# First q/k tiles uncast over two hardware DMA queues, first V through GpSimd, and scores in two PSUM tiles

## The chip, the cores and the metric

The kernel runs on one core of a Trainium2 chip. The core has TensorE (PE, with its weight loads shown as PEld), VectorE (DVE), ScalarE (ACT), GpSimd (POOL) and SyncE (SP). Each has its own queue of instructions, worked off in order; they meet at semaphores. Data come from HBM by DMA transfers, which GpSimd issues through a software queue and SyncE and ScalarE through hardware queues. A transfer issued by GpSimd may change the type on the way. The metric is the device time of one execution in microseconds.

## The reference, cut to what matters

```python
B, H, S, D = 8, 8, 576, 64           # q, k, v: [B, H, S, D], fp32
scores = q @ k.T / sqrt(D)           # masked: block of 64 rows i sees blocks j <= i
attn = exp(scores - max); attn /= sum(attn)
x = (attn @ v) as [B, S, 512]        # heads side by side
h = relu(x.T @ w_tok1) @ w_tok2      # 576 -> 256 -> 576, along the sequence
u = x + h.T
out = u + relu(u @ w_ch1) @ w_ch2    # 512 -> 1536 -> 512, along the channels
```

## The kernel before, in words

The kernel goes over eight batches b. For each it does attention in two head groups (hg) of four heads, then the token mix, then the channel MLP up and down. All products are in bf16 with fp32 sums.

**The planner.** Nothing is issued where it is written. Every step is an `Op` with the engines it may run on, an estimated cost, what it depends on, and a priority (lower goes first). `Plan.run` (L55) plays the work through with these estimates, a common DMA line (`xfer` is the estimated transfer time) and free lists of PSUM banks (`take`, `give`), and emits the steps in the order in which they start. That order is then the order of each engine's queue; the semaphores are set by the framework from what each instruction reads and writes.

**Loads.** `load_qk` (L245) fetches k and q of one head group: a transfer from GpSimd that casts to bf16 (`kraw`, `qraw`, rings of three), then one 32x32 block transpose on DVE into `kT` and `qT`. The 576 positions lie as 32 a x 18 k (`NB` = 18), so a transfer brings 18 rows of 64 to each of 128 partitions. `load_v` (L272) fetches V in five tiles of 128 positions (the last has 64), heads side by side, into `v1`, which also has a column of ones. For batch 0 the five tiles come uncast over ScalarE's hardware queue into `vstage` (L282), and DVE casts them (L292); for the others GpSimd's transfers cast (L286). After the first loads GpSimd sends the token weights (L305), the first and second halves of `wc1` (L324), and `wc2` (L333), with the loads of the next batches between them.

**Scores.** Per head group there are three sets of scores of up to 512 columns for each of four heads (`SETS`), transposed (keys on the partitions), each with a contraction of 32 twice (`par`). The PSUM tile `sc` has four banks, one for each head. For batch 0 a set is made in two halves, heads 0 and 1 and heads 2 and 3 (`halves`, with bank notes "sc01" and "sc23" in the planner); for the others a set is one step that takes both notes. ScalarE takes exp of two heads at a time into `e_sb` (L389). Small fills then zero the masked blocks on the diagonal (L428), for batch 0 on DVE or GpSimd. A last set of both head groups together, the tail, covers positions 512 to 575, into `et_sb`.

**AV.** For each head 15 products of the exponentials with V (L454) fill one bank; the column of ones gives the row sums, DVE inverts them (L475) and scales into `x_sb` (L481). In the planner the AV of every head depends on all the exponentials of its group, on the tail's and on V. The other steps (`token_mix` L532 to L654, `channel_up` L676, `channel_up_mixed` L703, `channel_down` L742) take a bank from `mm` (3) or `ups` (1); AV takes `ups` first.

Of the kernel before, what the change touches and what calls it, by code (L numbers as in the profile page):

```python
# [10 lines left out]
FP32 = mybir.dt.float32  # L11
# [104 lines left out]
def kernel(  # L116
# [11 lines left out]
    nc = tc.nc  # L128
# [36 lines left out]
    vstage = sb.tile([128, 5, DM], FP32, name="vstage")  # L165
# [16 lines left out]
    P.pool("ups", ups)  # L182
    P.pool("mm", mm)

    def bank_of(note):
        return (mm if note["pool"] == "mm" else ups)[note["slot"]]
# [51 lines left out]
    def warm_up():  # L238
        def emit(o):
            nc.scalar.activation(warm, nc.const_aps.tensor(0.0, (128, 1), FP32), EXP)  # L240

        P.add("ACT", 1.5, emit, (), -1e5)


    def load_qk(b, hg):  # L245
        i = (2 * b + hg) % 3
        prio = 10 * b + 4 * hg - (100 if b == 0 else 0)
        done = []
        for n, (src, raw, dst) in enumerate(((k, kraw[i], kT[i]), (q, qraw[i], qT[i]))):
            def emit_load(o, src=src, raw=raw):  # L250
                nc.gpsimd.dma_start(  # L251
                    out=raw.rearrange("p k d -> p (k d)"),
                    in_=src[b, 4 * hg : 4 * hg + 4].rearrange("h (p k) d -> (h p) (k d)", p=32),
                )

            load = P.add("POOL", 0.66, emit_load, reuse(("raw", n, i)), prio + n, xfer=8 * 0.191)

            def emit(o, raw=raw, dst=dst):
                nc.vector.transpose(  # L259
                    dst[:, 0:S, :]  # L260
                    .rearrange("p s e -> p (s e)")
                    .bitcast(I32)
                    .rearrange("p (a k) -> p k a", k=NB),
                    raw.rearrange("p k d -> p (k d)").bitcast(I32).rearrange("p (k a) -> p k a", k=NB),
                )

            op = P.add("DVE", dve_cost(576), emit, [load] + reuse(("T", n, i)), prio)
            reads(("raw", n, i), op)
            done.append(op)
        return done  # L270

    def load_v(b):  # L272
        t = v1[b % 2]
        war = reuse(("v", b % 2))
        done = []
        for J in range(5):
            p = 128 if J < 4 else 64

            def emit(o, J=J, p=p):
                src = v[b, :, 128 * J : 128 * J + p, :].rearrange("h p d -> p h d")  # L280
                if b == 0:
                    nc.scalar.dma_start(  # L282
                        out=vstage[0:p, J].rearrange("p (h d) -> p h d", h=H), in_=src
                    )
                else:
                    nc.gpsimd.dma_start(out=t[0:p, J, :, 0:64], in_=src)  # L286

            if b == 0:
                op = P.add("ACT", 0.5, emit, war, -1e4 + J, xfer=p / 2 * 0.018)

                def emit(o, J=J, p=p):
                    nc.vector.tensor_copy(  # L292
                        t[0:p, J, :, 0:64], vstage[0:p, J].rearrange("p (h d) -> p h d", h=H)
                    )

                op = P.add("DVE", dve_cost(512, 2), emit, [op], 2)
            else:
                op = P.add("POOL", 0.66, emit, war, 10 * b + (5.2 if b == 1 else 6) + 0.01 * J, xfer=p / 2 * 0.031)
            done.append(op)
        return done  # L300
# [48 lines left out]
    def score_set(b, parts, deps, war, prio, halves):  # L349

        ops = []
        for h0, h1 in halves:
            notes = [{"name": n} for n in ("sc01", "sc23")[h0 // 2 : h1 // 2]]

            def emit(o, h0=h0, h1=h1):
                for hg, c0, j0, i0, w in parts:
                    i = (2 * b + hg) % 3
                    for par in range(2):
                        for h in range(h0, h1):
                            r = slice(32 * h, 32 * h + 32)  # L360
                            nc.tensor.matmul(  # L361
                                out=sc[:, h, c0 : c0 + w],
                                lhsT=kT[i][r, j0 : j0 + 128, par],
                                rhs=qT[i][r, i0 : i0 + w, par],
                                start=(par == 0),
                                stop=(par == 1),
                            )
# [12 lines left out]
    def attention(b, ready, v_ready):  # L380
# [6 lines left out]
        def exp(dst, h0, h1, n, op, notes, prio):  # L387
            def emit(o):
                nc.scalar.activation(dst, sc[:, h0:h1, 0:n], EXP, scale=scale)  # L389

            return P.add("ACT", act_cost((h1 - h0) * n), emit, [op], prio, give=notes)

        def tail():
# [7 lines left out]
            exps = []  # L401
            for op, notes in score_set(b, parts, deps, war, prio, halves):
                h0 = 2 if notes[0]["name"] == "sc23" else 0
                exps.append(exp(dst[:, h0 : h0 + 2 * len(notes)], h0, h0 + 2 * len(notes), 128, op, notes, prio))
# [4 lines left out]
        for hg in range(2):  # L409
# [4 lines left out]
            exps = []  # L414
            for s, regions in enumerate(SETS):
                n = sum(w for _, _, _, w in regions)
                parts = tuple((hg,) + r for r in regions)
                these = []
                for op, notes in score_set(b, parts, ready[hg], e_war, prio + 0.1 * s, halves):
                    for note in notes:  # L420
                        h0 = 2 if note["name"] == "sc23" else 0
                        dst = e[:, h0 : h0 + 2, 512 * s : 512 * s + n]
                        these.append(exp(dst, h0, h0 + 2, n, op, [note], prio))
                exps += these
                for c in ((0,), (576,), (1024, 1344))[s]:
                    def emit(o, c=c, e=e):
                        engine = nc.vector if o.engine == "DVE" else nc.gpsimd
                        engine.memset(e[64:128, :, c : c + 64], 0.0)  # L428

                    exps.append(  # L430
                        P.add(
                            ("DVE", "POOL") if b == 0 else "DVE", {"DVE": dve_cost(128), "POOL": 0.4},
                            emit, these, prio,
                        )
                    )
# [4 lines left out]
            for h in range(4):  # L440
# [3 lines left out]
                def emit(o, h=h, head=head, bank=bank, hg=hg, e=e):  # L444
# [60 lines left out]
    def token_mix(b, x_done, w1_ready, w2_ready):  # L505
# [14 lines left out]
        for half in range(NH):  # L520
# [4 lines left out]
            for tts in ((0, 1),) if direct else ((0,), (1,)):  # L525
                bank = {}

                def emit(o, tts=tts, bank=bank, cols=cols):
# [13 lines left out]
                    take=[(("mm", "ups"), bank)],  # L542
# [12 lines left out]
            for m in range(NDM // NH * half, NDM // NH * (half + 1)) if direct else ():  # L555
                bank = {}

                def emit(o, m=m, bank=bank):
# [12 lines left out]
                    take=[(("mm", "ups"), bank)],  # L571
# [25 lines left out]
        for si in range(5):  # L597
            bank = {}

            def emit(o, si=si, bank=bank):  # L600
# [13 lines left out]
                take=[(("mm", "ups"), bank)],  # L614
# [15 lines left out]
        for si in range(4 * direct, 4 + odd):  # L630
            bank = {}

            def emit(o, si=si, bank=bank):
# [10 lines left out]
                "PE", mm_cost(128, 4), emit, deps, prio + 2 + 0.1 * si, take=[(("mm", "ups"), bank)]  # L644
# [23 lines left out]
    def channel_up(b, uT_done, wc1_ready, prio):  # L668
        g_war = reuse(("g", b % 2))
        done = []  # L670
        for cc in range(NDC):
# [12 lines left out]
            op = P.add("PE", mm_cost(512, 4), emit, uT_done + wc1_ready[cc] + g_war, prio + 0.1 * cc, take=[(("mm", "ups"), bank)])  # L684
# [8 lines left out]
    def channel_up_mixed(pair, umT_done, wc1_ready, prio):  # L693
        g_war = reuse(("gm", pair % 2))
        done = []
        for f in range(NDC // 4):
# [14 lines left out]
            op = P.add("PE", mm_cost(128, 16), emit, umT_done + wc1_ready[4 * f] + g_war, prio + 0.1 * f, take=[(("mm", "ups"), bank)])  # L711
# [14 lines left out]
    def channel_down(b, g_done, wc2_ready, u_done, prio, mixed=False):  # L726
# [3 lines left out]
        for n, si in enumerate(chunks):  # L730
# [8 lines left out]
            for part in range(3):  # L739
                def emit(o, part=part, c0=c0, bank=bank):  # L740
# [12 lines left out]
                    take=[(("mm", "ups"), bank)] if part == 0 else (),  # L753
# [92 lines left out]
```

## Time and profile before

| | |
|---|---|
| median of 3 runs | 342.0 us (341.95 to 346.04) |
| profiled execution, time / span | 343.53 us / 341.7 us |
| PE busy | 308.2 us, 90% of the span |
| DVE, ACT, POOL busy | 166.0, 163.3, 59.0 us |
| PE idle before its first product | 9.71 us |
| DMA, moved | 28.41 MB, 83 GB/s on the mean |

A profile is of one execution, and its times run from the start of the span. The page has the busy time of each engine, the span in 40 slices, the DMA queues, the chain of work that ended last, the costliest groups of instructions by source line, and the DMA issues with the time to landing. Views of the same trace answer closer questions: the timeline (instructions in order of time, merged, with the idle time before them and what released them), the windows (busy time in a stretch), the waits. A line as L361 is one of the kernel before. A group's mean time is that of one instruction; products are pipelined, so a busy TensorE need not be working at its full rate.

### The profile page before, as it was taken

The page shows a single profiled execution, that of the slowest core. Times are in us where ns is not written, and L with a number is a line of the kernel's source. Part 1 is how long each engine was busy: PE and PEld are TensorE (multiplying, and loading weights), DVE is VectorE, ACT ScalarE, POOL GpSimd, SP SyncE. Part 2 cuts the span into 40 slices and gives each one's busy share as a digit, 9 for nine tenths or more (in the row PEclk, how much of TensorE's full clock was granted, in tenths as well). Part 3 has the DMA queues.
Part 4 walks back from the last instruction along what each step waited for, and adds up shares of the span by engine and source line. Part 5 has one row for each costly group of instructions (what it writes and reads, how often), then busy time and mean ns, then how long its engine had stood idle before and what let it go on. Part 6 is the DMA issues. An engine that isn't in the chain of part 4 may idle for free.

```text
span 341.7 us, 7132 instructions
## 1 busy us (share of the span) xinstructions
PE 308.2 (90%) x3058; PEld 159.5 (47%) x3058; DVE 166.0 (49%) x367; ACT 163.3 (48%) x216; POOL 59.0 (17%) x97
## 2 busy tenths in 40 slices
PE   0356699999999898999998999999999999999994
PEld 0024444635455555545544554654454464444641
DVE  3513665767798849748666555514213212012012
ACT  1444367544676774564874576510541540532600
POOL 8444630151043151140040000000000000000000
PEclk9999989999999999999999999999999999999999
DMA  7999999097549396693090110003102003103013
GB/s 157 196 203 183 163 199 108 2 120 158 126 57 176 54 115 62 125 154 47 2 71 1 64 63 2 2 3 120 33 0 108 17 0 123 32 0 125 1 63 92
DMA packets 50832, 28.41 MB, mean 83 GB/s; under 512 B 38641, under 2 KB 42097, under 8 KB 50801
## 3 DMA queue, kind: packets, MB, share of 16 engines
q0 software_dynamic: 41120, 17.34, 42.3%
q1 hardware_dynamic: 4992, 9.44, 8.0%
q10 hardware_dynamic: 4688, 1.18, 2.1%
q8 instruction: 24, 0.39, 0.5%
q14 instruction: 8, 0.06, 0.0%
HBM read 35.85 MB, written 9.44 MB: 133 GB/s over the span
## 4 chain that ended last, share of the span: by engine, by line
PE 76%; DVE 11%; DMA 7%; ACT 2%; issue 2%; ACTq 1%; DVEq 0%
PE mm L742 26%; PE mm L676 23%; DMA vstage<-in_v_dram 7%; PE sc L361 7%; PE mm L532 5%; PE mm L703 3%; PE mm L454 3%; PE ups L454 3%; PE mm L603 2%; DVE u_sb L624 2%; DVE x_sb L481 2%; DVE qT L259 2%; ACT e_sb L389 1%; DVE kT L259 1%; PE mm L637 1%
## 5 line engine op out<-in xcount | busy, mean ns | idle before, releaser
L389 ACT ACTIVATE e_sb<-sc 128x1024 bf16<-128x1024 f32 x96 | 93.3, 1021 | 58.4 <-PE sc L361 57.6
L742 PE MATMUL mm<-wc_sb,gT 128*128 128x512 bf16 x384 | 87.9, 379 | 0.1
L676 PE MATMUL mm<-uT,wc_sb 128*128 128x512 bf16 x364 | 83.9, 379 | 0.6 <-DVE um_sb L624 0.5
L500 ACT ACTIVATE gT<-mm 128x512 bf16<-128x512 f32 x68 | 40.6, 597 | 73.6 <-PE mm L676 73.4
L676 PEld LDWEIGHTS <-wc_sb 128*128 128x128 bf16 x384 | 36.3, 98 | 46.3 <-issue 5.2
L361 PE MATMUL sc<-qT,kT 32*128 32x64 bf16 (+4 forms) x768 | 38.9, 297 | 20.7 <-DVE qT L259 12.1
L742 PEld LDWEIGHTS <-gT 128*128 128x128 bf16 x384 | 36.2, 98 | 42.5 <-issue 2.7
L758 DVE TENSOR_TENSOR o_sb<-mm,u_sb 128x512 f32<-128x512 f32 x32 | 22.1, 690 | 69.7 <-PE mm L742 69.1
L286 POOL DMA_DIRECT2D v<-in_v_dram x35 | 29.6, 858 | 47.1 <-PE mm L454 34.6
L454 PEld LDWEIGHTS <-e_sb 128*128 128x128 bf16 x896 | 32.5, 99 | 10.6 <-issue 7.1
L361 PEld LDWEIGHTS <-kT 32*128 32x128 bf16 x768 | 13.5, 96 | 41.8 <-issue 30.2
L259 DVE STREAM_TRANSPOSE kT<-kraw 128x576 int32<-128x576 int32 x16 | 20.0, 1251 | 7.4 <-DMA kraw<-in_k_dram 4.3
L454 PE MATMUL mm<-v,e_sb 128*128 128x65 bf16 x574 | 22.1, 195 | 0.9 <-DVE o_sb L758 0.9
L624 DVE TENSOR_TENSOR u_sb<-mm,x_sb 128x512 bf16<-128x512 f32 x24 | 15.8, 682 | 13.8 <-PE mm L603 13.7
L502 DVE TENSOR_SCALAR gT<-mm 128x512 bf16<-128x512 f32 x23 | 15.8, 688 | 12.2 <-PE mm L676 12.1
L481 DVE TENSOR_TENSOR x_sb<-mm,rinv 128x320 bf16<-128x320 f32 x41 | 19.7, 489 | 1.0
L259 DVE STREAM_TRANSPOSE qT<-qraw 128x576 int32<-128x576 int32 x16 | 19.8, 1237 | 0.7 <-DMA qraw<-in_q_dram 0.6
L428 DVE MEMSET e_sb<- 64x128 uint32 x61 | 9.7, 165 | 18.0 <-ACT e_sb L389 15.1
L532 PE MATMUL mm<-x_sb,w_sb 128*128 128x512 bf16 (+1 forms) x78 | 18.2, 376 | 0.0
L603 PE MATMUL mm<-aT,w_sb 128*128 128x512 bf16 x62 | 16.9, 381 | 0.0
L251 POOL DMA_DIRECT2D kraw<-in_k_dram x16 | 9.0, 560 | 39.9 <-DVE kT L259 32.8
L454 PE MATMUL ups<-v,e_sb 128*128 128x65 bf16 x322 | 14.5, 198 | 0.9 <-DVE x_sb L481 0.9
(68 smaller groups left out, 220.0 us busy)
## 6 DMA issues: line engine op xcount, KB each, us to landing
out_dram<-o_sb SPq DMA_DIRECT2D x16, 512.0 KB, 2.8
kraw<-in_k_dram POOLq DMA_DIRECT2D x16, 288.0 KB, 5.7
qraw<-in_q_dram POOLq DMA_DIRECT2D x16, 288.0 KB, 6.0
v<-in_v_dram POOLq DMA_DIRECT2D x28, 128.0 KB, 5.8
wc_sb<-in_moe_w_ch_dram POOLq DMA_DIRECT2D x8, 192.0 KB, 9.9
wc_sb<-in_moe_w_ch_dram POOLq DMA_DIRECT2D x3, 512.0 KB, 7.8
vstage<-in_v_dram ACTq DMA_DIRECT2D x4, 256.0 KB, 10.4
out_dram<-o_sb SPq DMA_DIRECT2D x8, 128.0 KB, 2.4
```

The lines of the kernel that those rows point to most:

```text
L259: nc.vector.transpose(dst[:, 0:S, :] .rearrange("p s e -> p (s e)") .bitcast(I32) .rearrange("p (a k) -> p k a", k=NB), raw.rearrange("p k ...
L286: nc.gpsimd.dma_start(out=t[0:p, J, :, 0:64], in_=src)
L361: nc.tensor.matmul(out=sc[:, h, c0 : c0 + w], lhsT=kT[i][r, j0 : j0 + 128, par], rhs=qT[i][r, i0 : i0 + w, par], start=(par == 0), stop=(p ...
L389: nc.scalar.activation(dst, sc[:, h0:h1, 0:n], EXP, scale=scale)
L454: nc.tensor.matmul(out=u[:, I, 0:65], lhsT=w, rhs=vt[:, J, head, 0:65], start=(J == 0), stop=(J == I),)
L481: nc.vector.tensor_tensor(out=xt[:, :, 64 * head : 64 * head + 64], in0=u[:, :, 0:64], in1=ri.to_broadcast([128, 5, 64]), op=MULT,)
L500: nc.scalar.activation(dst, src, RELU)
L532: nc.tensor.matmul(out=bank_of(bank)[:, W * n : W * n + W], lhsT=w[:, 128 * tt : 128 * (tt + 1)], rhs=xt[:, c, cols], start=(c == 0), stop ...
L603: nc.tensor.matmul(out=bank_of(bank), lhsT=w2_sb[:, t, c0 : c0 + 128], rhs=at[:, t, :], start=(t == 0), stop=(t == NDT - 1),)
L624: nc.vector.tensor_tensor(out=dst, in0=bank_of(bank)[r, :], in1=xt[r, si, :], op=ADD)
L676: nc.tensor.matmul(out=bank_of(bank), lhsT=wc1_sb[:, m, 128 * cc : 128 * (cc + 1)], rhs=uT[b % 2][:, m, :], start=(m == 0), stop=(m == NDM ...
L742: nc.tensor.matmul(out=bank_of(bank), lhsT=gt[:, cc, c0 : c0 + 128], rhs=wc2_sb[:, cc, :], start=(cc == 0), stop=(cc == NDC - 1),)
```

## The change

- `load_qk`: for batch 0, head group 0, k and q come uncast in two halves each (k 0 to 8 and 9 to 17 of `NB`), the first from SyncE's queue and the second from ScalarE's, into `gT[0]` read as fp32 (`stage[0]`); each half is cast by DVE or ScalarE into `kraw`/`qraw`. ScalarE's loading of its table moves behind these issues. For batches 0 and 1 each transpose is done in two halves.
- `load_v`: the five V tiles of batch 0 go from ScalarE's queue to GpSimd's, uncast, into `gT[1]` (`stage[1]`), behind k and q of head group 1; DVE or ScalarE casts them. `vstage` is gone.
- The PSUM tile `sc` of four banks becomes two tiles of two banks; `ups` (1) and `mm` (3) become `mm` (4).
- In the planner AV of a head depends on the exponentials and the tail's of its own half of the group. For batch 0 the zero fills are made for two heads each, twice as many, on DVE only.

```diff
+    stage = [t.rearrange("p c s -> p (c s)").bitcast(FP32) for t in gT]
...
-    sc = psum.tile([128, 4, 512], FP32, name="sc")
-    ups = ring(1, [128, 512], FP32, "ups", psum)
-    mm = ring(3, [128, 512], FP32, "mm", psum)
+    sc = ring(2, [128, 2, 512], FP32, "sc", psum)
+    mm = ring(4, [128, 512], FP32, "mm", psum)
...
-        P.add("ACT", 1.5, emit, (), -1e5)
+        P.add("ACT", 1.5, emit, (), -9e3)
...
+        parts = ((0, NB // 2), (NB // 2, NB)) if b < 2 else ((0, NB),)
...
+            loads = []
+            if not first:
+                def emit_load(o, hbm=hbm, raw2=raw2):
+                    nc.gpsimd.dma_start(out=raw2, in_=hbm)
+
+                loads = [P.add("POOL", 0.66, emit_load, raw_war, prio + n, xfer=8 * 0.191)]
+            for f, (k0, k1) in enumerate(parts):
+                if first:
+                    def emit_load(o, k0=k0, k1=k1, hbm=hbm, st=st):
+                        queue = nc.sync if o.engine == "SP" else nc.scalar
+                        queue.dma_start(out=st[:, D * k0 : D * k1], in_=hbm[:, D * k0 : D * k1])
+
+                    ld = P.add(("SP", "ACT")[f], 0.5, emit_load, (), -1e4 + n, xfer=8 * 0.092)
+
+                    def emit_cast(o, k0=k0, k1=k1, raw2=raw2, st=st):
+                        cast(o, raw2[:, D * k0 : D * k1], st[:, D * k0 : D * k1])
+
+                    ld = P.add(
+                        EVAC, {"ACT": act_cost(576), "DVE": dve_cost(576, 2)}, emit_cast, [ld], -1e4 + 2
+                    )
+                    reads(("g", 0), ld)
+                    loads = [ld]
...
+                op = P.add("DVE", dve_cost(32 * (k1 - k0), 0.54), emit, loads + T_war, prio + 0.1 * n)
...
-                if b == 0:
-                    nc.scalar.dma_start(
-                        out=vstage[0:p, J].rearrange("p (h d) -> p h d", h=H), in_=src
-                    )
-                else:
-                    nc.gpsimd.dma_start(out=t[0:p, J, :, 0:64], in_=src)
...
+                nc.gpsimd.dma_start(out=dst, in_=src)
+
+            prio = 10 * b + (2, 5.2, 6)[min(b, 2)] + 0.01 * J
+            op = P.add("POOL", 0.8, emit, war, prio, xfer=p / 2 * (0.018 if staged else 0.032))
+            if staged:
+                def emit(o, st=st, dst=dst):
+                    cast(o, dst, st)
+
+                op = P.add(
+                    EVAC, {"ACT": act_cost(512), "DVE": dve_cost(512, 2)}, emit, [op], 10 * b + 2
+                )
+                reads(("g", 1), op)
...
-                                out=sc[:, h, c0 : c0 + w],
+                                out=sc[h // 2][:, h % 2, c0 : c0 + w],
...
-                nc.scalar.activation(dst, sc[:, h0:h1, 0:n], EXP, scale=scale)
+                nc.scalar.activation(dst, sc[h0 // 2][:, :, 0:n], EXP, scale=scale)
...
+                    for f in (0, 1) if b == 0 else (None,):
+                        hs = slice(0, 4) if f is None else slice(2 * f, 2 * f + 2)
...
+                        op = P.add(
+                            "DVE", 0.1, emit, these[0] + these[1] if f is None else these[f], prio
+                        )
...
-                    exps + tail_done + v_ready + x_war + pads["e", ei],
+                    exps[h // 2] + tail_done[h // 2] + v_ready + x_war + pads["e", ei],
                     base + 4.5 if b == 0 else prio + 1,
-                    take=[(("ups", "mm"), bank)],
+                    take=[(BANK, bank)],
```

More of the change, by code (lines that the diff above doesn't have):

```diff
@@ L240, in emit, with cast @@
             nc.scalar.activation(warm, nc.const_aps.tensor(0.0, (128, 1), FP32), EXP)
-        P.add("ACT", 1.5, emit, (), -1e5)
+        P.add("ACT", 1.5, emit, (), -9e3)
+    EVAC = ("DVE", "ACT")
+    def cast(o, dst, src):
+        if o.engine == "ACT":
+            nc.scalar.copy(dst, src)
+        else:
+            nc.vector.tensor_copy(dst, src)
     def load_qk(b, hg):
         i = (2 * b + hg) % 3
+        first = b == 0 and hg == 0
         prio = 10 * b + 4 * hg - (100 if b == 0 else 0)
+        parts = ((0, NB // 2), (NB // 2, NB)) if b < 2 else ((0, NB),)
@@ L613, in token_mix @@
                 a_all + w2_ready + (um_free[pair] if si == 4 else u_war), prio + 1 + 0.1 * si,
[L614 removed]
+                take=[(BANK, bank)],
             )
@@ L752, in channel_down @@
                     "PE", mm_cost(512, 4), emit, deps, prio + 0.1 * n - 0.01 * part,
-                    take=[(("mm", "ups"), bank)] if part == 0 else (),
+                    take=[(BANK, bank)] if part == 0 else (),
                 )
```

93 lines of the change are left out of this document (41 added, 52 removed).

## The prediction

> **What bounds the kernel now.** The page comes first: the span, the busy times and the PE row of the 40 slices.
>
> ```profile
> span 341.7 us, 7132 instructions
> PE 308.2 (90%) x3058; PEld 159.5 (47%) x3058; DVE 166.0 (49%) x367; ACT 163.3 (48%) x216; POOL 59.0 (17%) x97
> PE   0356699999999898999998999999999999999994
> ```
>
> TensorE is 90% busy, and what it lacks lies in the first five slices of 8.5 us. The view of windows gives that in numbers (after the window and its length: PE, PEld, DVE, ACT, POOL busy, the granted clock, DMA share, GB/s).
>
> ```profile
> 0.00:10.00 10.00, 0.29 (x4) 0.24 (x8) 4.18 (x17) 1.49 (x2) 8.04 (x22) 1.00 0.84 164
> 10.00:20.00 10.00, 4.29 (x36) 1.36 (x31) 3.78 (x7) 5.01 (x5) 4.09 (x8) 1.00 1.21 197
> 20.00:30.00 10.00, 5.08 (x69) 2.57 (x67) 2.09 (x6) 3.73 (x5) 5.61 (x9) 1.00 1.15 205
> 30.00:40.00 10.00, 8.59 (x144) 6.32 (x144) 5.37 (x15) 5.05 (x6) 4.62 (x9) 1.00 1.55 150
> 50.00:60.00 10.00, 9.95 (x124) 4.54 (x124) 6.53 (x14) 7.67 (x11) 0.54 (x1) 1.00 0.99 117
> 200.00:240.00 40.00, 39.74 (x380) 21.48 (x379) 18.71 (x42) 16.37 (x24) 0.00 (x0) 1.00 0.07 27
> ```
>
> TensorE works 18.3 of the first 40 us, and 9.95 of 10 us at 50. So the kernel is a start of some 42 us, in which the first batch's attention runs nearly alone, and 300 us limited by TensorE. The timeline (start, busy time, engine, line, count, idle before it and its releaser) shows what fills the start.
>
> ```profile
> 6.58 1.26 DVE L259 STREAM_TRANSPOSE kT<-kraw 128x576 int32<-128x576 int32 x1 [3.96 <-DMA kraw<-in_k_dram]
> 8.40 1.26 DVE L259 STREAM_TRANSPOSE qT<-qraw 128x576 int32<-128x576 int32 x1 [0.56 <-DMA qraw<-in_q_dram]
> 9.71 1.05 PE L361 MATMUL sc<-qT,kT 32*128 32x512 bf16 x8 [9.71 <-DVE qT L259]
> 11.14 1.94 ACT L389 ACTIVATE e_sb<-sc 128x1024 bf16<-128x1024 f32 x2 [8.89 <-PE sc L361]
> 13.13 1.04 PE L361 MATMUL sc<-qT,kT 32*128 32x64 bf16 x8 [2.38 <-ACT e_sb L389]
> 14.21 1.02 ACT L389 ACTIVATE e_sb<-sc 128x1024 bf16<-128x1024 f32 x1 [1.12 <-PE sc L361]
> 15.28 1.03 PE L361 MATMUL sc<-qT,kT 32*128 32x64 bf16 x8 [1.11 <-ACT e_sb L389]
> 16.35 1.02 ACT L389 ACTIVATE e_sb<-sc 128x1024 bf16<-128x1024 f32 x1 [1.12 <-PE sc L361]
> 23.69 0.38 ACT L389 ACTIVATE et_sb<-sc 128x256 bf16<-128x256 f32 x1 [1.16 <-PE sc L361]
> 28.91 0.23 PE L454 MATMUL ups<-v,et_sb 128*128 128x65 bf16 x1 [2.87 <-DVE v L292]
> 34.18 1.94 ACT L389 ACTIVATE e_sb<-sc 128x1024 bf16<-128x1024 f32 x2 [1.19 <-PE sc L361]
> 41.66 1.04 PE L361 MATMUL sc<-qT,kT 32*128 32x512 bf16 x8 [2.42 <-DVE qT L259]
> ```
>
> The last row is batch 1's first scores. Three losses are to be seen. The first score waits until 9.71. Then TensorE and ScalarE take turns: a half set of scores from 13.13, its exponential from 14.21, the next half set only at 15.28, its exponential at 16.35, a period of 16.35 - 14.21 = 2.14 us for 1.02 us of ScalarE work. The half set at 15.28 writes heads 2 and 3, whose banks the exponential of 12.1 to 13.08 had long freed; it starts when the exponential of heads 0 and 1, in other banks of the same tile, ends at 15.23. So the whole four-bank tile is waited for, though the plan books its halves apart. Third, at 28.91 an AV product has waited 2.87 us for the last V cast, and the rest of the second head group's scores stands behind it.
>
> **The change, part by part.** I follow one mark, the end of the last exponential of batch 0, now 34.18 + 1.94 = 36.12.
>
> *First k and q.* Rows for it: the page's DMA issues (KB, median us to landing) and its queues (packets, MB, share).
>
> ```profile
> out_dram<-o_sb SPq DMA_DIRECT2D x16, 512.0 KB, 2.8
> kraw<-in_k_dram POOLq DMA_DIRECT2D x16, 288.0 KB, 5.7
> v<-in_v_dram POOLq DMA_DIRECT2D x28, 128.0 KB, 5.8
> q0 software_dynamic: 41120, 17.34, 42.3%
> q1 hardware_dynamic: 4992, 9.44, 8.0%
> q10 hardware_dynamic: 4688, 1.18, 2.1%
> ```
>
> Four transfers of 128 x 2304 B leave SP and ACT at about 0.8 us, 1.18 MB in all. The output queue q1, whose packets are nearly as long, moved 9.44 MB in 8.0% of 341.7 us, 345 GB/s, so 3.4 us of transfer; with the 1.3 us or so that its 512 KB took beyond 1.5 us of moving, q lands at 0.8 + 1.3 + 3.4 = 5.5 alone. If GpSimd's k and q of the second head group take half of the engines from 3.9 on, the last 1.6 us double and it is 7.1. I take 6.0. Then come a cast and two half transposes; a cast of 128x512 takes 0.41 (row below), so 0.46, and the two halves the 1.26 of a whole one, 0.15 of waits: 7.9 us. k comes ahead of q, and its cast and transposes (1.7 us) lie under q's transfer. First score at 8.0, 1.7 us earlier (0.7 to 2.3). ACT's table load moves behind two DMA issues and ends long before the first exponential.
>
> ```profile
> 14.47 0.41 DVE L292 CAST v<-vstage 128x512 bf16<-128x512 f32 x1
> ```
>
> The Trainium skill, "Trainium Kernel Development and Optimization", Key Constraints, speaks against this part: transfers from SP, ACT and GpSimd run on the same 16 engines, and several issuers save only issue time. By that rule the 1.7 would be near nothing and the sum 10.3 in place of 12.0; the rows, 2.8 us for 512 KB against 5.7 us for 288 KB, give the hardware queues more than that.
>
> *Two score tiles.* The first exponential waits for its own half: 14.21 - 13.13 = 1.08 after the scores start, not 11.14 - 9.71 = 1.43. It starts at 9.1. From there one half's scores run under the other's exponential. A tile's cycle is 1.08 + 1.02 + 0.05 = 2.15 and yields one half set; two tiles yield two, so 1.05 to 1.08 each, ScalarE being the limit. Head group 0: 6 x 1.05 = 6.3, to 15.4. The tail's two short exponentials (0.38 each, with their starts) 1.2, to 16.6, where now it is 23.69 + 0.38 = 24.07. **7.5 us** so far.
>
> *Head group 1* now takes 36.12 - 24.07 = 12.05. ScalarE alone needs 6 x 1.05 = 6.3. TensorE has six half sets and four AV products there. Rows for both paces:
>
> ```profile
> 30.90 0.95 PE L454 MATMUL ups<-v,e_sb 128*128 128x65 bf16 x14
> 32.66 0.10 PEld L361 LDWEIGHTS <-kT 32*128 32x128 bf16 x1
> 55.07 0.63 PE L361 MATMUL sc<-qT,kT 32*128 32x512 bf16 x8
> 58.90 0.60 PE L454 MATMUL ups<-v,e_sb 128*128 128x65 bf16 x14
> ```
>
> Two AV products lie between 30.90 and 32.66, 0.88 each; at 58.90 the same 14 matmuls take 0.60, and eight score matmuls 0.63 at 55.07 for 1.04 at 41.66. At the early pace that is 6 x 1.04 + 4 x 0.88 = 9.8 us, at the late one 6 x 0.63 + 4 x 0.60 = 6.2, and then ScalarE's 6.3 rules. I take 7.5, nearer to the late pace since TensorE will have been busy without a break from 8.0. Mark at 24.1 (22.9 to 26.4): **36.12 - 24.1 = 12.0 us** (9.7 to 13.2).
>
> The windows call the clock 1.00 in both stretches, so the pace is not in that column. The Trainium skill ("TensorE: Matmul & The Clock Gate", Why this matters for your kernels) says that TensorE reaches its full clock after about 4 us of dense work and loses it in a pause of 3 us: the pauses of 2.38 and 2.87 above would have kept it slow, and now wouldn't; by the rule the sum is 13.2.
>
> *V from GpSimd* goes behind k and q of group 1, which take the places of the present first pair (landed by 6.58 and 8.40). Its 4608 rows of 256 B are what q10 carries now; q10's packets took 2.1% x 16 x 341.7 / 4688 = 24.5 ns, GpSimd's mean 42.3% x 16 x 341.7 / 41120 = 56 ns. Over 16 engines that is 7.1 or 16.1 us, so V is there at 15.5 to 24.5. I take the lower, the row with this packet. AV of group 0 can't start before 16.6, so it costs nothing then, and the present 2.87 us stall goes (it is in the 12.05). At 24.5 it is a rival. The five casts (2 us of DVE, or ACT) lie in DVE's free time: 3.78 us busy of 10 at 10 to 20. Five issues more and two fewer on GpSimd cost 5 x 0.86 - 2 x 0.53 = 3.3 us ahead of the weights' issue (both durations in the next rows).
>
> *Does the later work find its data 12 us earlier?* A group of the page, rows of the timeline, and two of the chain that ended last (start, duration, what):
>
> ```profile
> L286 POOL DMA_DIRECT2D v<-in_v_dram x35 | 29.6, 858 | 47.1 <-PE mm L454 34.6
> 14.04 0.53 POOL L251 DMA_DIRECT2D qraw<-in_q_dram  x1 [1.64 <-DMA w_sb<-in_moe_w_tok_dram]
> 33.05 0.31 POOL L428 MEMSET e_sb<- 64x256 bf16 x1 [2.90 <-ACT e_sb L389]
> 33.30 2.24 POOL L333 DMA_DIRECT2D wc_sb<-in_moe_w_ch_dram  x3
> 45.93 0.88 POOL L286 DMA_DIRECT2D v<-in_v_dram  x1 [2.60 <-DMA wc_sb<-in_moe_w_ch_dram]
> 5.13 23.28 DMA vstage<-in_v_dram
> 67.11 1.89 PE mm L742 x8
> ```
>
> wc2 has landed at 45.9 and is first used at 67.11, so at 55 then: 9 us of slack for V's 3.3 to 7. Batch 1's q, issued at 14.04, at 17.3 then, with 5.7 of landing is there at 23; it is wanted two transposes (2.5) ahead of the scores at 41.66, at 39, then at 27. The zero fills of e go from GpSimd to DVE, so its queue no longer stands 2.90 us at 33.05; 16 short ones lie in DVE's idle time. Other edits I cost at nothing: four banks are still four banks, and from batch 1 a set still needs both tiles, so ScalarE's pairs (1.94) stay. TensorE's work past the mark is unchanged, and it is the bound: the 12.0 us come off the end. The profiled execution took 343.53 (span 341.7), which gives 331.5 and a span of 329.7; the median of the runs shown is 342.0, and 342.0 - 12.0 = **330.0**.
>
> **Rivals.**
>
> *A. The slow pace stays* through group 1: the mark is at 26.4, the gain 9.7, 332.3. For it: the early rows are all slow, even those of 30 to 40, where TensorE is busy for 8.59 us. Against: the pauses go. This includes the page's clock rule failing; the rule holding in full gives 342.0 - 13.2 = 328.8, and with the 2.42 us wait of 41.66 gone too, 326.4.
>
> *B. V lands at 24.5.* AV of group 0 stands in TensorE's queue ahead of some two sets of group 1's scores, so the mark is near 25 + 4 x 0.88 + 2.6 = 31: gain 5, 337. For it: GpSimd's packets are slower on the mean; against: most of those are casts or far longer.
>
> *C. The tile split does not separate the halves*: period 2.14 as now. Then only the start (1.7) and the V stall (2.9) are gained, 337.4. Against it: 15.28 waits for nothing but the tile.
>
> *D. Slower.* Everything that GpSimd sends after V comes late. If V's five transfers went one after another at the 5.8 us of the row for 128 KB, they would take 29 us from 8.4, 37.4 in place of the present 28.4 (5.13 + 23.28 in the chain): 9 us more, 351. It decides from V later than 28.4. Against: such transfers are issued 0.9 us apart now and overlap.
>
> **How the numbers follow.** Forecast with its faster end (326 to 331.5): 0.47; A (to 334): 0.21; B and C (334 to 339): 0.21; D: 0.06; more than 16 us gained: 0.05. The range 325.5 to 337.5 holds the first two, most of B and C and some of the last, about 0.85. Two per cent, 6.8 us, is about what a measurement of this kernel can tell from no change: faster means under 335.2. That is 0.47 + 0.21 + 0.05 and a little of B: 0.75; same 0.19; slower 0.06.
>
> **What would show it.** Right: first score at 7 to 9 us; exponentials of batch 0 about 1.05 us apart with no wait of 1.1 before each; V's last cast before 18; the last exponential of batch 0 at 23 to 26; batch 1's first scores by 30; windows past 60 as full as now. Wrong: half sets still 2.1 apart (C), an AV product waiting for a cast past 20 (B), TensorE waiting at 25 to 55 on batch 1's k and q or on weights, or PE windows emptier later by more than 3 us because the plan's order came out worse.

## The result, and the profile after

| | before | after |
|---|---|---|
| median (4 runs each) | 344.02 us (341.95 to 346.91) | 330.92 us (330.77 to 331.52) |
| profiled execution, span | 341.7 us | 329.1 us |
| ratio, 95% interval | | 0.9617 (0.9526 to 0.9707) |

Forecast were 330.0 us and a span of 329.7. (The median of before was 342.0 when the sum was made; its later runs lie higher, and the sum is best compared by the spans: 12.0 us forecast, 12.6 measured.) Ratios, here and below, leave out the few executions that ran over 1.5% longer than the fastest of the same kernel. The sum came out; three of its terms did not, as the marks of the timelines will show. First the page of the kernel after: span, busy times, PE by slices.

```profile
span 329.1 us, 7174 instructions
PE 304.7 (93%) x3016; PEld 159.1 (48%) x3058; DVE 159.8 (49%) x376; ACT 171.9 (52%) x237; POOL 61.2 (19%) x97
PE   0599998999999999999999999999999999999994
```

The busy time of TensorE hardly changed (308.2 to 304.7; the second trace lacks 42 of the 3058 matmuls, so it is a little short); what went is for the most part idle time in the first slices. The windows of the kernel after, columns as before:

```profile
0.00:10.00 10.00, 0.00 (x0) 0.10 (x1) 4.40 (x19) 3.97 (x6) 8.76 (x20) 1.00 0.86 230
10.00:20.00 10.00, 7.09 (x70) 2.75 (x70) 4.71 (x17) 6.87 (x9) 5.72 (x13) 1.00 1.20 202
20.00:30.00 10.00, 10.00 (x142) 6.48 (x140) 4.11 (x17) 6.12 (x7) 7.05 (x10) 1.00 1.20 205
30.00:40.00 10.00, 9.86 (x101) 5.45 (x99) 8.61 (x21) 5.98 (x8) 5.78 (x8) 1.00 1.64 190
50.00:60.00 10.00, 8.79 (x116) 4.69 (x116) 6.80 (x19) 4.47 (x5) 0.77 (x2) 1.00 0.57 86
```

From 20 to 40 us TensorE is full, where before it was only from 50 on. In 50 to 60 it now lacks 1.2 us, nearly all of it one wait of 1.15 us for a zero fill. The first ten are emptier than before. The timeline says why:

```profile
5.02 1.24 ACT L249 CAST kraw<-gT 128x576 bf16<-128x576 f32 x2 [1.87 <-DMA gT<-in_k_dram]
5.72 0.72 DVE L290 STREAM_TRANSPOSE kT<-kraw 128x288 int32<-128x288 int32 x1 [3.11 <-ACT kraw L249]
6.39 1.24 ACT L249 CAST qraw<-gT 128x576 bf16<-128x576 f32 x2
7.97 1.79 DVE L290 STREAM_TRANSPOSE kT<-kraw 128x288 int32<-128x288 int32 x3 [1.53 <-DMA kraw<-in_k_dram]
9.61 2.32 DVE L290 STREAM_TRANSPOSE qT<-qraw 128x288 int32<-128x288 int32 x4
10.90 1.05 PE L389 MATMUL sc<-qT,kT 32*128 32x512 bf16 x8 [10.90 <-DVE qT L290]
14.12 1.94 ACT L417 ACTIVATE e_sb<-sc 128x1024 bf16<-128x1024 f32 x2 [0.21 <-PE sc L389]
16.26 1.94 ACT L417 ACTIVATE e_sb<-sc 128x1024 bf16<-128x1024 f32 x2 [0.21 <-PE sc L389]
16.27 0.42 DVE L251 CAST v<-gT 64x512 bf16<-64x512 f32 x1
18.68 0.38 ACT L417 ACTIVATE et_sb<-sc 128x256 bf16<-128x256 f32 x1 [0.20 <-PE sc L389]
24.25 1.03 PE L389 MATMUL sc<-qT,kT 32*128 32x64 bf16 x8
25.21 0.95 PE L486 MATMUL mm<-v,e_sb 128*128 128x65 bf16 x14
27.23 1.94 ACT L417 ACTIVATE e_sb<-sc 128x1024 bf16<-128x1024 f32 x2 [0.88 <-PE sc L389]
28.78 0.59 PE L486 MATMUL mm<-v,e_sb 128*128 128x65 bf16 x14
```

The casts of k are done at 6.26 and those of q at 7.63, but DVE stands until 7.97 on GpSimd's k: its queue has head group 1's k between the two halves of the first k. The first scores start at 10.90. From there two half sets take 16.26 - 14.12 = 2.14 us, not one. V's last cast ends at 16.7, before anything wants it. In group 1 half sets of 1.03 and AV products of 0.95 alternate on a full TensorE, until the pace rises at 28.

The marks, in us from the start of the span:

| mark | before | after | gained by then | in this step |
|---|---|---|---|---|
| first scores start | 9.71 | 10.90 | -1.19 | -1.19 |
| tail's exponentials end (group 0) | 24.07 | 19.06 | 5.01 | 6.20 |
| last exponential of batch 0 ends | 36.12 | 29.17 | 6.95 | 1.94 |
| batch 1's first scores start | 41.66 | 33.90 | 7.76 | 0.81 |
| first channel-up product | 47.71 | 36.63 | 11.08 | 3.32 |
| last output issued | 337.56 | 325.02 | 12.54 | 1.46 |

The prediction put the whole gain ahead of the third mark. 6.95 of it lies there and 5.6 behind.

### The profile page after: what moved, and what is told of

Same layout as the page of the kernel before. It is cut to its first block, busy times and chain, and to the rows that moved or that the text cites. A ratio compares the mean times of both kernels' runs of the same rounds, so it can differ in the third digit from the quotient of the medians.

```text
span 329.1 us, 7174 instructions
## 1 busy us (share of the span) xinstructions
PE 304.7 (93%) x3016; PEld 159.1 (48%) x3058; DVE 159.8 (49%) x376; ACT 171.9 (52%) x237; POOL 61.2 (19%) x97
## 4 chain that ended last, share of the span: by engine, by line
PE 84%; DVE 8%; issue 3%; ACT 2%; DMA 2%; POOLq 0%
PE mm L774 27%; PE mm L708 25%; PE sc L389 9%; PE mm L486 7%; PE mm L564 5%; PE mm L635 4%; PE mm L735 3%; ACT e_sb L417 2%; DMA kraw<-in_k_dram 2%; DVE u_sb L656 2%; PE mm L669 2%; DVE x_sb L513 2%; DVE qT L290 1%; DVE kT L290 1%; DVE rinv L507 1%
## 5 line engine op out<-in xcount | busy, mean ns | idle before, releaser
L708 PE MATMUL mm<-uT,wc_sb 128*128 128x512 bf16 x369 | 87.8, 379 | 1.1 <-issue 0.3
L532 ACT ACTIVATE gT<-mm 128x512 bf16<-128x512 f32 x78 | 46.5, 598 | 76.6 <-PE mm L708 76.3
L486 PE MATMUL mm<-v,e_sb 128*128 128x65 bf16 x896 | 34.0, 196 | 1.2 <-DVE e_sb L459 1.2
L513 DVE TENSOR_TENSOR x_sb<-mm,rinv 128x320 bf16<-128x320 f32 x64 | 30.5, 489 | 1.5
L656 DVE TENSOR_TENSOR u_sb<-mm,x_sb 128x512 bf16<-128x512 f32 x32 | 20.7, 684 | 8.9 <-PE mm L635 7.3
L290 DVE STREAM_TRANSPOSE kT<-kraw 128x576 int32<-128x576 int32 (+1 forms) x20 | 20.2, 1032 | 6.0 <-ACT kraw L249 3.1
L459 DVE MEMSET e_sb<- 64x128 uint32 (+1 forms) x72 | 10.5, 153 | 19.7 <-ACT e_sb L417 17.0
L290 DVE STREAM_TRANSPOSE qT<-qraw 128x576 int32<-128x576 int32 (+1 forms) x20 | 19.8, 1020 | 0.1
L507 DVE RECIPROCAL rinv<-mm 128x5 f32<-128x5 f32 x64 | 10.6, 179 | 14.4 <-PE mm L486 14.2
L686 DVE COPY uT<-mm 128x512 bf16<-128x512 bf16 x17 | 6.6, 420 | 16.6 <-PE mm L669 16.3
```

The lines of the kernel that those rows point to most:

```text
L290: nc.vector.transpose(dst[:, 0:S, :] .rearrange("p s e -> p (s e)") .bitcast(I32) .rearrange("p (a k) -> p k a", k=NB)[:, k0:k1], raw2.bit ...
L486: nc.tensor.matmul(out=u[:, I, 0:65], lhsT=w, rhs=vt[:, J, head, 0:65], start=(J == 0), stop=(J == I),)
L513: nc.vector.tensor_tensor(out=xt[:, :, 64 * head : 64 * head + 64], in0=u[:, :, 0:64], in1=ri.to_broadcast([128, 5, 64]), op=MULT,)
L532: nc.scalar.activation(dst, src, RELU)
L656: nc.vector.tensor_tensor(out=dst, in0=bank_of(bank)[r, :], in1=xt[r, si, :], op=ADD)
L708: nc.tensor.matmul(out=bank_of(bank), lhsT=wc1_sb[:, m, 128 * cc : 128 * (cc + 1)], rhs=uT[b % 2][:, m, :], start=(m == 0), stop=(m == NDM ...
```

## The experiments

Theory 1 at first: splitting the score tile is the largest part, V's earlier landing the second, the hardware queues for q and k bring nothing as built. Theory 2: V out of TensorE's way is the largest part. "Before" was timed anew beside each group of runs, with medians of 344 to 345.4 us. The groups did not all run on one chip, so where two kernels of different groups differ by some 2 us, the marks of their traces are given too.

### Undoing one part: u_sc, u_v, u_v_sp, u_qk

```diff
 u_sc
-    sc = ring(2, [128, 2, 512], FP32, "sc", psum)
+    sc = psum.tile([128, 4, 512], FP32, name="sc")
...
```

> The changed kernel with one part undone: the scores are one PSUM tile of four banks again; the planner's order of instructions is the same as in the changed kernel. Theory 1 (the split is the largest part of the gain): in head group 0 the half sets are 2.14 us apart again instead of 1.07, 5 to 6 us more up to the tail's end; in head group 1 AV products fill the turns, so 0 to 2 us more there; 336 to 339 us. Theory 2 (taking V's late landing out of TensorE's queue is the largest part): 332 to 334 us.

Measured: 337.32 us (336.85 to 337.52), 6.4 more than the kernel after. Its timeline:

```profile
14.69 1.02 ACT L417 ACTIVATE e_sb<-sc 128x1024 bf16<-128x1024 f32 x1 [1.12 <-PE sc L389]
15.77 1.03 PE L389 MATMUL sc<-qT,kT 32*128 32x64 bf16 x8 [1.11 <-ACT e_sb L417]
16.84 1.02 ACT L417 ACTIVATE e_sb<-sc 128x1024 bf16<-128x1024 f32 x1 [1.12 <-PE sc L389]
```

The turns are back, 2.15 us for one half set, with the same instructions in the same order. Group 0 ends at 24.56 for 19.06, and the 5.5 us stay in every later mark: last exponential 35.04 for 29.17, last output 331.70 for 325.02. So the wait was the tile's, not the banks', and here, with V in time, what is won at the start goes through to the end.

```diff
 u_v
-                nc.gpsimd.dma_start(out=dst, in_=src)
+                (nc.scalar if staged else nc.gpsimd).dma_start(out=dst, in_=src)
 u_v_sp
+                (nc.sync if staged else nc.gpsimd).dma_start(out=dst, in_=src)
...
```

> The changed kernel with one part undone: the first V comes over ScalarE's hardware queue into a staging tile of its own again, behind the first k and q. Theory 1: V's rows share the engines packet by packet with GpSimd's long ones as before, the last tile lands at 25 to 29 us, AV of head group 0 waits in TensorE's queue with scores behind it; 334 to 337 us. Theory 2: this wait is most of the gain, 338 to 341 us. A third reading, that V's queue does not matter: 331 us.

Measured: 351.02 us, beyond every expectation. The timeline of u_v shows a cause that I had not thought of:

```profile
1.67 21.95 ACTq L316 DMA_DIRECT2D vstage<-in_v_dram  x5
23.65 1.28 ACT L241 ACT_TABLE_LOAD   x1 [23.65 <-issue]
25.06 0.65 ACT L250 CAST kraw<-gT 128x576 bf16<-128x576 f32 x1
27.66 1.05 PE L389 MATMUL sc<-qT,kT 32*128 32x512 bf16 x8 [27.66 <-DVE qT L291]
```

V's five issues, placed ahead of the table load, held ScalarE's queue for 21.95 us, and the casts of k and q stood behind them. So this run's time says nothing of what a late V costs. With SyncE as the issuer no computing engine is held:

> As the undoing of V's queue before, but V goes over SyncE's hardware queue behind the first halves of k and q, so no computing engine's queue holds its issues. Theory 1 (a hardware queue's V lands late, since its 256 B rows alternate with GpSimd's long ones): first scores as in the changed kernel, last V cast at 23 to 29 us, AV of head group 0 waits 5 to 9 us in TensorE's queue; 335 to 339 us. Rival (the 351 us were all due to ScalarE's queue being held by the issues): V is there by 18, 330 to 332 us.

Measured: 349.36 us (348.95 to 349.54), longer than expected and longer than before. Its first scores are where they should be (10.53). Rows of its timeline, and of its DMA issues (KB, median us to landing):

```profile
22.05 0.43 DVE L252 CAST v<-vstage 128x512 bf16<-128x512 f32 x1 [8.47 <-DMA vstage<-in_v_dram]
33.15 0.67 PE L486 MATMUL mm<-v,e_sb 128*128 128x65 bf16 x9 [2.19 <-DVE e_sb L459]
33.71 0.62 ACT L250 CAST v<-vstage 64x512 bf16<-64x512 f32 x1 [15.60 <-DMA vstage<-in_v_dram]
```

```profile
vstage<-in_v_dram SPq DMA_DIRECT2D x4, 256.0 KB, 21.7
```

and of the kernel after:

```profile
gT<-in_v_dram POOLq DMA_DIRECT2D x4, 256.0 KB, 8.6
```

The same rows of V take 21.7 us from a hardware queue and 8.6 from GpSimd's. The pages also differ in their queues (packets, MB, share), u_v_sp first, then the kernel after:

```profile
q0 software_dynamic: 40832, 16.75, 40.9%
q1 hardware_dynamic: 9968, 11.21, 10.9%
```

```profile
q0 software_dynamic: 41200, 17.93, 44.4%
q1 hardware_dynamic: 5280, 10.03, 8.8%
```

With V, GpSimd's queue has 368 packets and 1.18 MB more; on SyncE's queue the same V is 4688 packets. So the hardware queue sends V in its rows of 256 B, and GpSimd's sends it in packets of 3.2 KB on the mean. The Trainium skill ("DMA: Bandwidth & Descriptors", Queues, rings and completion order) has it that an engine takes turns between its queues packet by packet. By that rule a packet of one row would get one turn for each of GpSimd's longer ones; the landing times and the packet counts fit it, but no view here shows the turns themselves. The place in GpSimd's queue is thus what lets V land in time, and Theory 2 is nearer than I had it. The undoing overstates it, though: here the last of V lands at 33.7, behind k and q, where before the change it came first on its queue and landed at 28.4. And its casts, placed for an early V, hold up DVE's queue (8.47 us at 22.05) and ScalarE's (15.60 at 33.71), with zero fills and the tail's second exponential behind them.

```diff
 u_qk
-        first = b == 0 and hg == 0
+        first = False
```

> The changed kernel with one part undone: the first k and q come cast over GpSimd's queue again, ahead of head group 1's and of V (the half transposes stay). In the changed kernel the first scores start at 10.90 us, later than before (9.71). Theory 1 (this part brings nothing as built, because the casts stand one after another on ScalarE and head group 1's k is transposed between the two halves of k): first scores at 9.5 to 11, V 3 us later, 330 to 332.5 us. Rival (it frees GpSimd's queue for V and so carries part of the gain): 333 to 336 us, with AV waiting for V's casts.

Measured: 331.70 us (330.66 to 332.07), the kernel after within 1 us. First scores at 9.11, 1.8 us earlier than with the hardware queues, and the last output is issued at 325.08 for 325.02. As built, this part of the change brings nothing that can be told.

### One part alone on the kernel before: x_sc, x_v

```diff
 x_v
-                    nc.scalar.dma_start(
+                    nc.gpsimd.dma_start(
-                op = P.add("ACT", 0.5, emit, war, -1e4 + J, xfer=p / 2 * 0.018)
+                op = P.add("POOL", 0.8, emit, war, 2 + 0.01 * J, xfer=p / 2 * 0.018)
```

x_v is V from GpSimd alone. x_sc is the two score tiles alone, the reverse of u_sc's lines.

> The kernel before with one part done alone: the scores in two tiles of two banks (the tail's exponentials in two). Theory 1 (the split and V's earlier landing are worth little without each other): head group 0 ends 5 to 6 us earlier, at 18 to 19, but AV then waits for the last V cast, still at 28, in front of group 1's scores; only 1 to 4 us gained: 339 to 342 us (against before at 342 to 346). Rival (the gains add): 6 us or more gained, 336 to 338 us.

> The kernel before with one part done alone: the first V uncast from GpSimd, behind k and q of both head groups (staging tile kept). Theory 1: the wait of 2.9 us at 28.91 goes and group 1 follows at once, but the half sets stay 2.14 apart; 3 to 6 us gained, 337 to 340 us. Rival (the gains add up to the whole 13 with the split's 6): 7 us gained, 335 to 337 us.

Measured: x_sc at a ratio to before of 0.9942 (0.9902 to 0.9982), 2.0 us less; x_v 336.33 us against 344.26, ratio 0.9777 (0.9737 to 0.9816), 7.9 us less, which is its rival's figure. The timeline of x_sc:

```profile
18.78 0.38 ACT L389 ACTIVATE et_sb<-sc 128x256 bf16<-128x256 f32 x1 [0.20 <-PE sc L361]
29.43 0.42 DVE L292 CAST v<-vstage 64x512 bf16<-64x512 f32 x1 [3.85 <-DMA vstage<-in_v_dram]
31.98 1.94 ACT L389 ACTIVATE e_sb<-sc 128x1024 bf16<-128x1024 f32 x2 [10.34 <-PE sc L361]
41.86 0.63 PE L361 MATMUL sc<-qT,kT 32*128 32x512 bf16 x8 [2.43 <-DVE qT L259]
```

Group 0 ends at 19.16, five us earlier, and ScalarE then stands 10.34 us because AV waits for V at 29.43, with group 1's scores behind it. At the last exponential of batch 0 (36.42 for 36.12) nothing of the five us is left. What this trace gains at its end, the last output at 336.30 for 337.56, arises behind it: batch 1's first scores wait as before (2.43 us), but then take 0.63 and not 1.04. Alone the split brings 2.0 us, with V in time 6.4; V alone 7.9. The wait that takes its place swallows the split, and Theory 1's ranking falls: V's move is what the rest depends on.

V's move brings more than the 2.87 us stall, though. The timeline of x_v:

```profile
8.31 1.05 PE L361 MATMUL sc<-qT,kT 32*128 32x512 bf16 x8 [8.31 <-DVE qT L259]
```

The first scores come 1.40 us earlier than before with k and q still whole and from GpSimd: k's transpose starts at 5.49 for 6.58. So most of what the prediction put down to the hardware queues for k and q comes with V leaving ScalarE's queue, where it had run beside them. Group 1 takes 8.92 us for 12.05.

### The order of the transposes: z_order

```diff
+        behind = qk[0, 0] if b == 0 and hg == 1 else []
-                op = P.add("DVE", ..., emit, loads + T_war, prio + 0.1 * n)
+                op = P.add("DVE", ..., emit, loads + T_war + behind, prio + 0.1 * n)
```

> The changed kernel, with the transposes of batch 0's head group 1 made to depend on those of head group 0, so that DVE does not wait for GpSimd's k (landed at 7.95) between the halves of the first k. Theory 1: the first scores start at 8.3 to 8.8 instead of 10.90 and the 2.1 to 2.6 us reach the end: 328.4 to 329 us. Rival: they are lost on the way (AV of group 0 waits for V, whose last cast ended at 16.7, or the weights set the pace): 330 to 331 us.

Measured: 328.86 us (328.38 to 329.45), 2.1 better than the kernel after.

```profile
8.22 1.05 PE L390 MATMUL sc<-qT,kT 32*128 32x512 bf16 x8 [8.22 <-DVE qT L291]
```

That is the 8.0 of the prediction; the 2.68 us were lost to DVE's queue order (10.52 to 10.91 in u_sc, u_v_sp and u_dep, which have the old order). By the medians 2.06 of them reach the end, by the last outputs (323.62 for 325.02) 1.40.

### The pace: z_warm

```diff
+            for _ in range(16):
+                nc.tensor.matmul(out=sc[1][:, 1, :], lhsT=um_sb[1][:, 0:128], rhs=um_sb[1], start=True, stop=True)
...
```

> The changed kernel with the transposes in order (as z_order) and 16 products of zeros, 128x128 by 128x512, ahead of the first scores on TensorE, from 2 to 8 us; their result is not used. Theory 1 (TensorE runs at half pace in group 0 and 1 because it was idle before, and can be brought to full pace ahead): half sets of 0.6 us, AV of 0.6 us, group 1 limited by ScalarE at 1.05 us each, the last exponential of batch 0 some 3 us earlier than in z_order (27.1): 325 to 327 us. Rival (the pace falls again while scores of 32-row products alternate with exponentials): AV products of 0.95 us in group 1 as now; 328 to 330 us.

Measured: 329.30 us (329.19 to 329.45), no better than z_order. Timeline and windows of z_warm:

```profile
8.18 0.64 PE L398 MATMUL sc<-qT,kT 32*128 32x512 bf16 x8 [0.92 <-DVE qT L299]
13.07 1.95 PE L398 MATMUL sc<-qT,kT 32*128 32x320 bf16 x16 [1.60 <-ACT e_sb L426]
23.09 0.95 PE L495 MATMUL mm<-v,e_sb 128*128 128x65 bf16 x14
```

```profile
10.00:20.00 10.00, 7.40 (x85) 3.47 (x85) 3.59 (x16) 7.47 (x10) 6.30 (x13) 0.60 1.21 203
20.00:30.00 10.00, 9.95 (x120) 6.82 (x119) 4.68 (x18) 4.99 (x6) 6.79 (x10) 0.54 1.18 206
```

The rival holds. The first scores run at 0.64, and by 13 the fast pace is lost again, with no wait for ScalarE over 1.60 us; the granted clock falls to 0.54 in 20 to 30, where AV takes 0.95. So slow pace and low clock go together. In the kernel after the same stretch shows 1.00 at the same 0.95. The kernel before does both: 1.00 to 40 us, and in the window that the prediction did not show, after AV had once run at 0.59 (36.83) and TensorE had waited 2.42 us, a low clock:

```profile
40.00:50.00 10.00, 8.06 (x62) 3.86 (x66) 5.89 (x12) 4.46 (x5) 5.30 (x8) 0.83 1.38 199
```

In these traces the column told of the slow clock only after it had once been fast.

### What the plan's dependency is worth: u_dep, and whole sets: z_full

```diff
 u_dep
-                    exps[h // 2] + tail_done[h // 2] + v_ready + x_war + pads["e", ei],
+                    exps[0] + exps[1] + tail_done[0] + tail_done[1] + v_ready + x_war + pads["e", ei],
 z_full (on z_order)
-                ... score_set(b, parts, ready[hg], e_war, prio + 0.1 * s, halves):
+                ... score_set(..., halves if hg == 0 else ((0, 4),)):
```

> The changed kernel with one part undone: in the planner AV of a head depends on all exponentials of its group and of the tail again. No instruction is added or removed; TensorE's order goes back nearly to that of before (two AV together and a whole set of scores, and batch 1's first scores ahead of the second half of token mix). Theory 1 (5.6 of the 12.6 us arose after the last exponential of batch 0, by this order): batch 1's first scores wait some 2 us for the transposes, the first channel-up product comes 4 to 6 us after them instead of 2.73; 333 to 336 us. Rival (that gain came from weights or V landing in time, whatever the order): 330 to 332 us.

Measured: 328.70 us (328.51 to 328.99): 2.2 *better* than the kernel after, so the theory's number is wrong. It was half right: batch 1's first scores (31.76) do come ahead of token mix's second half again and channel-up follows 4.59 us later, not 2.73. But the mark before it falls from 29.17 to 27.45. The timeline of u_dep in group 1:

```profile
20.92 0.96 PE L486 MATMUL mm<-v,e_sb 128*128 128x65 bf16 x14
21.86 1.06 PE L389 MATMUL sc<-qT,kT 32*128 32x64 bf16 x16
22.94 1.94 ACT L417 ACTIVATE e_sb<-sc 128x1024 bf16<-128x1024 f32 x2 [1.38 <-PE sc L389]
```

Here the two halves of a set stand together, and 16 matmuls of four heads take 1.06 us, where the kernel after pays 1.03 for 8 of two heads, twice, with an AV product between. In a stretch limited by TensorE that is a loss, 1.72 us at the mark. By the first channel-up product 0.28 of it is left (36.35 for 36.63), and at the last output the lead is 1.90 (323.12): the plan came out otherwise further on as well, so this run alone does not show that the 2.2 us are those of the half sets.

> The changed kernel with the transposes in order (z_order), and head group 1 of batch 0 made in whole sets of four heads instead of halves, so TensorE has 3 sets of 1.06 us there instead of 6 halves of 1.03. Theory 1 (group 1 is limited by TensorE at half pace): the last exponential of batch 0 comes 0.5 to 2 us earlier than in z_order (27.14); 327 to 328.5 us. Rival (with whole sets ScalarE waits for each set again, and that takes back as much): 328.5 to 331 us.

Measured: 328.50 us (327.77 to 329.60), z_order within the spread. Its mark is at 28.62, later than z_order's 27.14, as the plan also put token mix's products in front of the second and third sets. Its time decides nothing. Its trace shows that with whole sets the pace rose sooner (ten token mix products in 1.25 us at 22.24, in z_order 2.32 at 25.34) and that it was lost again behind a wait of 1.91 us (AV 0.96 at 29.43).

### Both repairs: z_best, and without the hardware queues: z_best_noq

> The changed kernel with both repairs: the transposes of head group 1 behind those of group 0 (z_order, 2.1 us better than the changed kernel) and AV made to depend on the whole group again (u_dep, 2.2 us better). Theory 1 (they cost at different places, before group 0 and in group 1, so they add): first scores at 8.2 to 8.6, the last exponential of batch 0 at 24.5 to 25.5, 326 to 327 us. Rival (from there on something else, as V or the weights, holds TensorE): 328 to 329 us, with TensorE waiting on DVE or on a transfer between 20 and 40 us.

Measured: 326.44 us (326.26 to 327.90), ratio to before 0.9440 (0.9403 to 0.9476), 4.5 us below the kernel after. The repairs add (2.1 + 2.2). First scores at 8.16 and, from the timeline, the last exponentials:

```profile
20.97 3.88 ACT L418 ACTIVATE e_sb<-sc 128x1024 bf16<-128x1024 f32 x4 [1.39 <-PE sc L390]
21.69 0.59 PE L487 MATMUL mm<-v,e_sb 128*128 128x65 bf16 x14
```

The mark is at 24.85, and AV runs at the fast pace from 21.69. z_order differs from z_best in AV's dependency alone; its mark is at 27.14, and its AV is still slow later:

```profile
28.30 0.96 PE L487 MATMUL mm<-v,e_sb 128*128 128x65 bf16 x14
```

In both traces TensorE waits nowhere from 16.3 on up to these products. So whole sets with AV in pairs reached the fast pace after 5.4 us of unbroken work, and half sets in turn with AV had not after 12. The dependency thus costs pace, and not only 1.03 twice for 1.06; why half sets in turn with AV stay slow for so long is not shown. Here the lead stays: 2.29 us at the mark, 2.49 at the first channel-up product (34.73 for 37.22), 3.03 at the last output.

> As z_best, with the first k and q cast over GpSimd's queue again, as before the change. Theory 1 (the two hardware queues are worth about what they bring forward the first scores, 9.11 in u_qk against 8.22 in z_order): 327 to 328 us, 0.5 to 1.5 us more than z_best. Rival (they are worth nothing, as V lands sooner or the plan fits better without them): within 0.3 us of z_best or below it.

Measured: 330.49 us (329.14 to 331.63), 4.05 more than z_best, but not for the reason expected: first scores at 8.22, the mark 0.9 us *earlier* (23.95), the first output issued at 60.17 for 65.15, and only then behind, the seventh of the 24 at 184.62 for 175.73. The plan came out otherwise and lost later what it had won. What the hardware queues are worth of themselves stays open; the start gives them 0.1 us here.

## Why the prediction was right, point by point

The time, the range and the sign held. By steps:

- **First scores at 8.0** was wrong: 10.90. The landing was right (q issued at 1.2, 5.2 to 5.4 us to landing, so 6.6 for my 6.0). The step that failed is the cast and two half transposes that were to end at 7.9: it took DVE's queue as free between the halves. I counted what is issued and not what it is moved past, head group 1's k, whose wait for GpSimd's transfer stands in line. z_order gives 8.22. That the hardware queues bring this start forward was wrong too: x_v has 8.31 without them.
- **Half sets 1.05 us apart** was right: 1.07, and group 0 from the first exponential to the tail's end 19.06 - 11.97 = 7.09 for my 7.5. u_sc shows the cause.
- **Group 1 in 7.5 us** was wrong in size: 10.11, beyond the slow end of my range (9.8). The pace was the slow one (rival A), and the reason that I gave for the fast one, dense work from 8.0, does not hold: TensorE is dense from 18.25 and AV still takes 0.95 at 25.21. The Trainium skill ("TensorE: Matmul & The Clock Gate", Why this matters for your kernels) asks for some 4 us of dense work and for no pause of over some 3 us. These products bear out neither half: z_order's 12 us without a wait did not bring the fast pace, and z_warm lost it with no wait over 1.60. Nor were the early rows of before all slow, as Rival A has it: AV takes 0.59 at 36.83.
- **V in time** was right: the last cast runs from 16.27 to 16.69, TensorE not waiting. The price was luck. It took 4608 packets of one row at 24.5 ns; from GpSimd V came in some 368 longer packets (the queues beside u_v_sp).
- **"TensorE's work past the mark is unchanged"** was wrong, by +5.6 us, and made up for the two shortfalls. Rows of before, then of after, for its largest piece:

```profile
42.63 2.31 PE L532 MATMUL mm<-x_sb,w_sb 128*128 128x256 bf16 x10
47.71 1.03 PE L676 MATMUL mm<-uT,wc_sb 128*128 128x512 bf16 x4
```

```profile
32.20 1.25 PE L564 MATMUL mm<-x_sb,w_sb 128*128 128x256 bf16 x10
36.63 1.03 PE L708 MATMUL mm<-uT,wc_sb 128*128 128x512 bf16 x4
```

  Before, the pace was lost behind the 2.42 us wait ahead of 41.66, and token mix's ten products took 2.31; after, they take 1.25 and stand ahead of batch 1's scores, over the transposes. u_dep, with before's order at the fast pace, needs 4.59 from those scores to channel-up: so of the 3.32 us, 6.05 - 4.59 = 1.46 go with the pace and 4.59 - 2.73 = 1.86 with the order. The wait need not cost the pace: x_sc has one of 2.43 us there and keeps it. The last 1.46 us, spread over the 290 us behind, I can't assign.
- **The AV dependency at nothing** was wrong: it costs about 2.2 us (u_dep; 2.4 from z_order to z_best), since the plan then takes half sets apart, which run one by one and at the slow pace for longer.
- Rival C is excluded by the 2.14 us for two half sets, B and D by V's landing. The data for later work were in time, as computed: after its first scores TensorE waits for no transfer in the trace.

A right total from wrong terms is luck: two shortfalls of 2.9 and 2.6 us, 0.4 more in group 0 than forecast, and a windfall of 5.6.

## What to carry to other kernels

A wait that two halves of one tile share in the framework can cost a whole alternation of two engines: look for an instruction that waits for a reader of banks or columns that it does not touch, and give the halves tiles of their own. What such a split wins is lost if the next thing in line is a transfer, so move that first. When a step is cut in parts or moved, read the order of each queue that it goes through: a part that waits for a transfer between two parts that don't is a stall, and a finer dependency may make a planner separate products that ran together on different rows.

## What the hardware showed that I had not expected

- Issuing V's five transfers from ScalarE's hardware queue held ScalarE for 21.95 us (u_v); issued from SyncE they hold no one who computes, and a tile still takes 21.7 us to land (u_v_sp).
- The same V was 4688 packets on a hardware queue and 368 on GpSimd's, where a tile landed after 8.6 us.
- Half sets on 64 of the 128 rows cost 1.03 us alone, a whole set of both halves 1.06 (u_dep). In turn with AV they also kept TensorE at the slow pace for over 12 us of unbroken work (z_order), whole sets for 5.4 (z_best).
- At the slow pace the window's clock column may read 1.00 (the kernel after, 20 to 30 us) or 0.54 (z_warm); the duration of a known product is the safer sign (14 AV matmuls: 0.95 or 0.59 us).
